# Units 8 to 23 of a recurrence: scores and state stacked into one matmul, one TensorE task per unit

## The chip, the cores and the metric

The program runs on one core of a Trainium2 chip. The metric is device microseconds of that core: 506.9 before (median of 3 runs, 506.85 to 506.91). Below, TensorE is the matmul engine, VectorE, ScalarE and GpSimd the three others that compute, and SyncE (SP) issues most DMAs. SBUF is the memory on the chip, PSUM the eight accumulator banks that TensorE writes.

## The reference

```python
B, H, S, D = 4, 8, 768, 48                 # batch, heads, time, head size
for t in range(S):                         # per batch and head: a 48 x 48 state
    y[t]  = r[t] @ (state + outer(u * k[t], v[t]))
    state = w[t][:, None] * state + outer(k[t], v[t])
x = y as [3072 tokens, 384]
h = x @ w_in                               # 384 x 2048
out = elu(h) @ w_out                       # 2048 x 384
```

All in float32. The decay w lies between 0.8 and 0.95.

## The kernel before, in words

**The recurrence** is computed in blocks of time. There are NU = 24 units. Units 0 to 3 ("whole") are one batch and 128 steps; units 4 to 23 are two batches (halves h = 0, 1, on token rows 0 to 63 and 64 to 127) and 64 steps, and alternate between two pairs of batches, so that unit i + 2 needs the state that unit i leaves. For a unit VectorE makes the running products of w (`e_scan`, `g_scan`) and scales k and r with them (`hats`). Heads stand in four pairs p; q is the head in a pair, on partitions 0 to 47 and 64 to 111.

Of a unit of 64 steps TensorE then computes two tasks. The *score* task `("s", i)` (function `score`): four transposes of k into bank pb (they become `kt`, ScalarE), 16 score matmuls k by r into pa, and the first half of the part of y that comes from the state (`state_part`, 16 matmuls st by r). VectorE writes the scores over the diagonal in tile `am`, where a mask allows it (`mask`; the diagonal, r k u, is spread out by GpSimd in `spread`). The *value* task `("v", i)` (`value`): 32 matmuls of v by am, the second half of the state part, all accumulated in one y, and 16 matmuls kt by v for the state's update. Units 22 and 23 (`last`) have neither transposes nor update. Then y is copied out in two parts, xh (ScalarE) and xl (VectorE, the rest), and the update is added to the state `st` (`update`), which is scaled for unit i + 2 by `scale_state`. A matmul that reads 48 or 64 partitions and writes 32 or 64 uses only a tile of TensorE's 128x128 array (64x32, 64x64), and matmuls in different tiles run side by side. In the trace an fp32 matmul is two instructions (a transpose is one).

**The two layers** run in 6 chunks of 512 tokens, four units each. A step f of 16 is a task g1 (9 matmuls of 128x512, weights and x in two parts each) and a task g2 (9 more); between them ScalarE and VectorE compute the elu (lines 269 to 283). Chunk 0 begins in plain fp32 while the weights are unpacked on ScalarE and VectorE.

**The order** is written out by a planner in the program (class `Plan`): each task has an engine, a cost (`COST`), what it comes after, buffers that it holds (`hold`, `SLOTS`) and, for some, a due time (`BEGINS`, the planned starts of the chunks, and `NUDGE`, a shift for single tasks). The engines get their tasks in the order in which the planner's own clock starts them, and each engine, and SP's queue of DMAs, works through its list in order. Units of chunk c + 1 are thus mixed into the steps of chunk c, and loads start `LEAD` us ahead of their chunk's planned start.

PSUM: three banks acc for the second layer, two ph for the first, two pa, one pb.

Of the kernel before, what the change touches and what calls it, by code (L numbers as in the profile page):

```python
# [20 lines left out]
P = 128  # L21
C = 128
# [25 lines left out]
def _pieces():  # L48
    res = []
    for h in range(H):  # L50
        s, e = h * D, (h + 1) * D
        while s < e:
# [12 lines left out]
            gh=0.62, sp=1.4, s=1.64, s0=1.6, s2=1.1, v=1.95, v0=1.6, v2=1.3, g=2.04, g32=2.65, out=0.6)  # L65
# [4 lines left out]
BEGINS = (21.0, 116.0, 196.0, 274.0, 351.0, 427.0, 493.0)  # L70
# [8 lines left out]
LEAD = 69.5  # L79
# [3 lines left out]
SLOTS = dict(wx=1, w=2, k=3, rk=2, v=3, eg=2, md=2, am=2, kt=2, pa=1, pb=1, wg=2, ph=2, m=2, gh=2, gl=2, x=2, acc=1, raw0=1, raw1=1, x0=1, x1=1, x1a=1, x1b=1)  # L83

LEADS = dict(ld="ld_w ld_k ld_v ld_rk ld_wx", es="es gs", rh="rkc rh kh pc sc", sp="rk rku md pd sp", fl="fl", s="s mk kt", v="v xf xh xl up", raw="raw", a="a",
             cc="cand cs cb cc cx sg", wl="wh wl wt wl1 wh1", g1="g1 r1 r2 stt", g2="g2 gh gl")
NUDGE = dict(a={1: -20.75, 2: -37.25},
             cc={1: -10, 2: -20.25, 6: 56.75, 8: -22, 11: 6, 12: 5.75, 14: -4.75, 15: 1.5},
             es={2: -12.5, 4: 3, 6: 3.5, 7: 13.5, 13: -11.5, 16: -1.75, 20: 3.75},
             g1={3: -1.25, 4: 21, 5: 16.5, 31: -17.25, 37: 70.75, 46: 48.25, 47: -20.75, 48: -0.5, 58: -15.25, 76: -6.25, 80: -9.25, 84: -11.5, 94: -11.75},  # L90
             g2={3: 88.5, 18: 4.25, 19: 14.25, 20: -1.5, 26: -11.5, 33: -5.25, 34: -2.75, 42: 0.25, 43: 6, 48: 24, 54: 7.5, 79: -12.75, 83: -8.5, 84: -17.5, 85: 16.75, 87: -4.25, 94: 6.75, 99: 51.75},
             ld={5: -17.75},
             raw={2: -71.5},
             rh={2: -16, 4: -9.75, 8: -40, 9: -5.5, 17: 42, 19: 17.75},
             s={1: -4.25, 12: 31.25, 17: 10},
             sp={1: 13.25, 6: 3.25, 13: -19.75, 19: -3.25, 23: -6},
             v={8: 24.25, 15: -15.5, 16: -18.25},
             wl={1: -22.25, 8: 15.75, 12: -2.25})
# [3 lines left out]
class Plan:  # L102
# [16 lines left out]
    def order(self):  # L119
# [36 lines left out]
        while len(order) < len(ts):  # L156
            moved = False
            for e in ready:
# [18 lines left out]
                for p, n, us in self.holds.get(k, ()):  # L177
                    at_, n_ = ring[p][0], len(ring[p][1])
                    ring[p][0] = (at_ + n) % n_
                    for x in range(n):  # L180
                        ring[p][1][(at_ + x) % n_] = True
                    if p in turn:
                        turn[p].pop(0)
                        if not turn[p]:
                            del turn[p]
                    h = [p, [(at_ + x) % n_ for x in range(n)], set(us) | {k}]
                    if p == "pa":
# [139 lines left out]
def rwkv_elu_kernel(ctx, tc, wkr, rk, vp, u, uz, gkrw, gv, gu, wraw, out):  # L327
# [39 lines left out]
    xf = xp.tile([P, NK, N], F32, name="xf")  # L367
# [30 lines left out]
    def pair(u_):  # L398
        if u_["i"] in SPARE:
            return spare()[0:2]  # L400
        t = ps_a.tile([P, 2, N], F32, tag="pa", name="pa", bufs=1)
        return [t[:, q] for q in range(2)] if u_["whole"] else t

    def single():
        return ps_a.tile([P, 512], F32, tag="pb", name="pb", bufs=1)
# [14 lines left out]
    def load(u_, n):  # L420
        i = u_["i"]
        if n in WKR:
            lo, hi = WKR[n]
            t, src = ld.tile([R2, hi - lo], F32, tag=n, name=n, bufs=SLOTS[n]), wkr[i, :, lo:hi]
        elif n == "wx":
            t, src = ld.tile([R2, W1], F32, tag=n, name=n, bufs=SLOTS[n]), wkr[i, :, 0:W1]
        elif n == "rk":
            t, src = ld.tile([P, 2, DM], F32, tag=n, name=n, bufs=SLOTS[n]), rk[i]
        else:
            t, src = ld.tile([P, 4 * P], F32, tag=n, name=n, bufs=SLOTS[n]), vp[i]  # L430
# [54 lines left out]

    def spread_act(u_):
        u_["am"] = am = at.tile([P, 2, NP, u_["L"]], F32, tag="am", name="am", bufs=SLOTS["am"])
        for q in range(2):
            for p in range(NP):
                act(am[:, q, p], ident if u_["whole"] else ident_h, AF.Copy, scale=u_["md"][:, q, p:p + 1])  # L490

    def spread_dve(u_):
        u_["am"] = am = at.tile([P, 2, NP, u_["L"]], F32, tag="am", name="am", bufs=SLOTS["am"])
# [3 lines left out]
    def spread(u_):  # L497
        u_["am"] = am = at.tile([P, 2, NP, L], F32, tag="am", name="am", bufs=SLOTS["am"])
        for lo in range(0, P, L):
            rs = slice(lo, lo + L)  # L500
            nc.gpsimd.affine_select(out=am[rs].rearrange("t q p s -> t (q p) s"),  # L501
                                    in_=u_["md"][rs].rearrange("t q p -> t (q p)").unsqueeze(2).broadcast_to([L, NS, L]),
                                    pattern=[[0, NS], [1, L]], compare_op=ALU.is_equal,
                                    fill=0.0, base=0, channel_multiplier=-1)

# [12 lines left out]
    def score(u_):  # L518
        if not u_["last"]:
            u_["pt"] = pt = single()[:, 0:NP * R2].rearrange("t (p d) -> t p d", p=NP)  # L520
            for p in range(NP):
                nc.tensor.transpose(pt[:, p], u_["k"][:, p, :], ident[0:R2, 0:R2])  # L522
        both = pair(u_)
        n = NP * u_["L"]
        if u_["whole"]:
            u_["pa"] = pa = [t[:, 0:n].rearrange("t (p s) -> t p s", p=NP) for t in both]
        else:
            u_["pa"] = both[:, :, 0:n].rearrange("t q (p s) -> t q p s", p=NP)
            pa = [u_["pa"][:, q] for q in range(2)]
        for p in range(NP):  # L530
            for lo in range(0, C, u_["L"]):
                for q in range(2):
                    rs, ts = slice(64 * q, 64 * q + D), slice(lo, lo + u_["L"])
                    nc.tensor.matmul(pa[1 - q][ts, p], u_["k"][rs, p, ts], u_["r"][rs, p, ts], start=True, stop=True)  # L534
        if u_["whole"]:
            u_["pu"] = both[1][0:R2, 0:NP * D].rearrange("d (h p e) -> d h p e", h=1, p=NP)
            u_["py"] = both[0][:, 0:NK * C].rearrange("d (h k t) -> d h k t", h=1, k=NK)
        else:
            u_["pu"] = both[0:R2, :, 0:NP * D].rearrange("d h (p e) -> d h p e", p=NP)
# [3 lines left out]
    def mask(u_):  # L543
        if u_["whole"]:
            for q in range(2):
                nc.vector.copy_predicated(u_["am"][:, q], above[u_["L"]][:, q], u_["pa"][q])
        else:
            nc.vector.copy_predicated(u_["am"], above[u_["L"]], u_["pa"])
# [9 lines left out]
    def value(u_):  # L558
        v, am, kt, whole = u_["v"], u_["am"], u_.get("kt"), u_["whole"]
        rows = [slice(0, C)] if whole else [slice(L * h, L * h + L) for h in range(2)]  # L560
        for n, (p, x) in enumerate(VALUES):
            for h, rs in reversed(list(enumerate(rows))):
                job(u_, h, p, x, v[rs, P * p + 32 * x:P * p + 32 * x + 32], am[rs, 1 - x // 2, p],
                    start=(whole and n < 4), stop=(whole and n >= len(VALUES) - 4))
        if not whole:
            state_part(u_, 0, u_["last"])
        if u_["last"]:
            return
        for p in range(NP):
            for z in range(2):  # L570
                lo = 64 * z
                for h, rs in enumerate(rows):
                    nc.tensor.matmul(u_["pu"][lo:lo + D, h, p], kt[rs, p, lo:lo + D], v[rs, P * p + 80 * z:P * p + 80 * z + D],  # L573
                                     start=whole, stop=(whole or p == NP - 1))
# [103 lines left out]
    for u_ in units:  # L678
# [37 lines left out]
        add(("s", i), "PE", K["s0" if u_["whole"] else "s2" if u_["last"] else "s"], lambda u_=u_: score(u_), [("rh", i), ("const",)] + [("sp", i)] * (i > 1) + before, due=DUE.get(i))  # L716
        add(("mk", i), "DVE", K["mk0" if u_["whole"] else "mk"], lambda u_=u_: mask(u_), [("s", i), ("sp", i)])
        if not u_["last"]:
            add(("kt", i), "ACT", K["kt"], lambda u_=u_: trans_out(u_), [("s", i)])
        after = [("mk", i), ("kt", i), ("ld_v", i)]  # L720
        if i % B:
            after.append(("v", i - 1))
        add(("v", i), "PE", K["v0" if u_["whole"] else "v2" if u_["last"] else "v"], lambda u_=u_: value(u_), after,
# [30 lines left out]
    for c in range(NC):  # L754
# [3 lines left out]
        for f, lo, hi in steps[c]:  # L758
# [17 lines left out]
            if c == NC - 1 and final:  # L776
# [11 lines left out]
                add(("g2", n - 1), "PE", g * 2 / 3 * CUT / N, lambda x=x, y=y: rest(x, y, a, lambda: pair(units[-1])[:, 0], "a"), [("g2a", 2)], due=due)  # L788
# [23 lines left out]
    for u_ in units:  # L812
        i, c = u_["i"], u_["c"]
        for n, users in dict(w=["es", "gs"] + ["fl"] * (i >= LATE), k=["s", "v"], rk=["md"], v=["v"], wx=["fl"]).items():
            hold(n, ("ld_" + n, i), [(x, i) for x in users])
        hold("eg", ("es", i), [("rh", i), ("pc", i)])
# [5 lines left out]
        hold("pb", ("s", i), [("kt", i)], fifo=False)  # L822
        hold("kt", ("s", i), [("v", i)])
        if i not in SPARE:
# [10 lines left out]
    for c in range(NC):  # L835
        hold("raw0", ("out", c, 0), [("store", c, m) for m in range(NK)])
    add(("least",), "DVE", 0.5, least, [(n, i) for i in range(NU) for n in ("fl", "pc")], due=BEGINS[-2] + 10.0)
    add(("guard",), "PE", 0.2, guard, [("least",)], due=BEGINS[-2] + 14.0)
    add(("verdict",), "DVE", 0.35, verdict, [("guard",)], due=BEGINS[-2] + 18.0)
    hold("pb", ("guard",), [("verdict",)], fifo=False)  # L840
    with tc.manual_schedule():
        for t in plan.order():
            warm(FILL.get(t["key"], 0))
# [138 lines left out]
```

## Time and profile before

| | |
|---|---|
| median of 3 runs | 506.9 us |
| the profiled execution | 507.46 us, its span (first to last instruction) 505.7 us |
| TensorE busy | 496.8 us (98%), granted clock 1.0 throughout |
| VectorE, ScalarE, GpSimd busy | 339.0 (67%), 271.4 (54%), 41.2 us (8%) |
| DMA | 51.09 MB in 18738 packets, 33% of the 16 engines' time on the main queue |

The profile is one execution. An engine is busy while one of its instructions runs; matmuls overlap, so a TensorE that is always busy need not be at its peak, and starts say more than durations. In a row of the timeline the first number is the start, the second the time until the last of the group has ended. Line numbers are those of the kernel before.

### The profile page before, as it was taken

What the parts mean: (1) busy time and instruction counts of PE and PEld (TensorE: products, weight loads), DVE (VectorE), ACT (ScalarE), POOL (GpSimd) and SP (SyncE); (2) the same over time, 40 slices, a digit from 0 to 9 for tenths busy, and PEclk for the clock granted to TensorE, in tenths of its full rate; (3) what the DMA queues carried; (4) which work ended last, traced back from release to release, by engine and by line L of the source; (5) the groups of instructions that cost most, each with busy time, mean ns of one, the idle gap of its engine ahead of it and who ended that gap; (6) DMA issues with size and microseconds to landing.
All of it is one profiled execution on the core that took longest, in us unless ns stands there. A gap on an engine that the chain in (4) does not pass through costs nothing.

```text
span 505.7 us, 13790 instructions
## 1 busy us (share of the span) xinstructions
PE 496.8 (98%) x6038; PEld 409.1 (81%) x6038; DVE 339.0 (67%) x509; ACT 271.4 (54%) x526; POOL 41.2 (8%) x54
## 2 busy tenths in 40 slices
PE   8999999999999999999899999999999999999996
PEld 7887888887888788888788888888888887888885
DVE  7999999995997524899432799533799543333332
ACT  4999576657554425655643645444644444445352
POOL 2000000013111100112000031100021100000000
PEclk9999999999999999999999999999999999999999
DMA  8977935204813100844390242230332000100001
GB/s 256 335 229 241 298 128 187 78 4 162 222 50 108 41 3 1 242 128 113 85 249 17 81 121 71 71 98 1 121 100 60 3 0 3 64 3 0 1 0 66
DMA packets 18738, 51.09 MB, mean 101 GB/s; under 512 B 2288, under 2 KB 2416, under 8 KB 18672
## 3 DMA queue, kind: packets, MB, share of 16 engines
q1 hardware_dynamic: 18240, 49.36, 32.7%
q8 instruction: 49, 0.80, 0.6%
q10 hardware_dynamic: 432, 0.79, 0.4%
q14 instruction: 17, 0.14, 0.1%
HBM read 45.42 MB, written 4.72 MB: 99 GB/s over the span
## 4 chain that ended last, share of the span: by engine, by line
PE 88%; DVE 5%; DMA 4%; issue 1%; ACT 1%; DVEq 0%; ACTq 0%
PE acc L296 35%; PE ph L265 34%; PE pa L508 6%; DMA wx<-in_wkr_dram 3%; PE acc L293 3%; PE ph L261 2%; PE pa L534 2%; PE pa L573 2%; PE acc L415 1%; PE pb L522 1%; DVE eg L441 1%; ACT wx L460 1%; DVE eg L451 1%; DMA w<-in_wkr_dram 1%; DVE m L275 1%
## 5 line engine op out<-in xcount | busy, mean ns | idle before, releaser
L275 DVE SCALAR_TENSOR_TENSOR m<-m,ph 128x512 f32<-128x512 f32 (+2 forms) x104 | 66.5, 641 | 82.5 <-ACT m L272 82.2
L269 ACT ACTIVATE m<-ph 128x512 f32<-128x512 f32 (+2 forms) x104 | 58.5, 563 | 92.6 <-PE ph L265 85.2
L265 PE MATMUL ph<-xh,w_l 128*128 128x512 f32 x270 | 105.3, 390 | 0.0
L296 PE MATMUL acc<-gh,w_l 128*128 128x512 f32 x268 | 104.5, 390 | 0.0
L283 DVE TENSOR_TENSOR gl<-m,gh 128x512 fp32r<-128x512 f32 x90 | 62.6, 696 | 42.7 <-ACT gh L279 42.5
L279 ACT CAST gh<-m 128x512 fp32r<-128x512 f32 x90 | 55.7, 619 | 51.5 <-DVE m L275 29.8
L296 PE MATMUL acc<-gh,w_h 128*128 128x512 f32 x180 | 71.8, 399 | 0.0
L265 PE MATMUL ph<-xh,w_h 128*128 128x512 f32 x180 | 71.3, 396 | 0.0
L296 PE MATMUL acc<-gl,w_h 128*128 128x512 f32 x180 | 70.2, 390 | 0.0
L265 PE MATMUL ph<-xl,w_h 128*128 128x512 f32 x180 | 70.1, 389 | 0.0
L272 ACT ACTIVATE m<-m 128x512 f32<-128x512 f32 (+2 forms) x104 | 62.2, 599 | 2.1
L265 PEld LDWEIGHTS ph<-xh,w_l 128*128 128x128 f32 x270 | 50.7, 188 | 10.7
L296 PEld LDWEIGHTS acc<-gh,w_l 128*128 128x128 f32 x268 | 50.3, 188 | 10.7
L501 POOL TENSOR_SCALAR_AFFINE_SELECT am<-md 64x512 f32<-64x512 f32 x32 | 30.3, 947 | 248.7 <-DVE md L470 203.0
L265 PEld LDWEIGHTS ph<-xh,w_h 128*128 128x128 f32 x180 | 33.8, 188 | 7.9 <-DVE m L275 0.6
L296 PEld LDWEIGHTS acc<-gh,w_h 128*128 128x128 f32 x180 | 33.8, 188 | 7.8
L265 PEld LDWEIGHTS ph<-xl,w_h 128*128 128x128 f32 x180 | 33.8, 188 | 6.7
L296 PEld LDWEIGHTS acc<-gl,w_h 128*128 128x128 f32 x180 | 33.8, 188 | 6.5
L265 PE MATMUL ph<-xh,w_g 128*128 128x512 f32 x90 | 36.1, 402 | 0.0
L265 PE MATMUL ph<-xl,w_g 128*128 128x512 f32 x90 | 35.1, 390 | 0.0
L296 PE MATMUL acc<-gh,w_g 128*128 128x512 f32 x88 | 35.1, 398 | 0.0
L296 PE MATMUL acc<-gl,w_g 128*128 128x512 f32 x88 | 34.4, 391 | 0.0
(115 smaller groups left out, 689.1 us busy)
## 6 DMA issues: line engine op xcount, KB each, us to landing
wraw<-in_wraw_dram SPq DMA_DIRECT2D x16, 768.0 KB, 7.1
k<-in_wkr_dram SPq DMA_DIRECT2D x24, 448.0 KB, 6.3
rk<-in_rk_dram SPq DMA_DIRECT2D x20, 384.0 KB, 4.4
v<-in_vp_dram SPq DMA_DIRECT2D x24, 256.0 KB, 7.1
w<-in_wkr_dram SPq DMA_DIRECT2D x24, 227.9 KB, 4.1
out_dram<-o SPq DMA_DIRECT2D x15, 256.0 KB, 2.3
wx<-in_wkr_dram SPq DMA_DIRECT2D x8, 227.9 KB, 3.3
out_dram<-o ACTq DMA_DIRECT2D x3, 256.0 KB, 2.6
```

The source lines that it names most:

```text
L261: nc.tensor.matmul(ph, w_f[f][:, 0, k], x_[2][:, k], start=(k == 0), stop=(k == NK - 1))
L265: nc.tensor.matmul(ph, w[f][:, 0, k], y[:, k], start=(k == n == 0), stop=(k == NK - 1 and n == 2))
L269: act(s["m"], s["ph"], AF.Relu, scale=-1.0)
L272: act(s["m"], s["m"], AF.Exp, scale=-1.0)
L275: stt_(s["m"], s["m"], -1.0, s["ph"], ALU.add, ALU.max)
L279: nc.scalar.copy(s["gh"], s["m"])
L283: nc.vector.tensor_tensor(s["gl"], s["m"], s["gh"].bitcast(F32), ALU.subtract)
L293: nc.tensor.matmul(a_, w_f[f][:, 1, m], fold(s, s["m"][:, a:b]), start=first, stop=final)
L296: nc.tensor.matmul(a_, w[f][:, 1, m], fold(s, g[:, a:b]), start=(first and n == 0), stop=(final and n == 2))
L501: nc.gpsimd.affine_select(out=am[rs].rearrange("t q p s -> t (q p) s"), in_=u_["md"][rs].rearrange("t q p -> t (q p)").unsqueeze(2).broadc ...
L508: nc.tensor.matmul(u_["py"][32 * j:32 * j + 32, h, k], l, r, **flags)
L534: nc.tensor.matmul(pa[1 - q][ts, p], u_["k"][rs, p, ts], u_["r"][rs, p, ts], start=True, stop=True)
```

## The change

For units 8 to 23 (`STACK = 8`) the state part and the values become one matmul. A tile `stack` holds for each half h the 64 rows of v and, on 48 of the other 64 partitions, the scaled state; the 16 rows between are zero (`clear`). The tile am (now `ams`, double width) holds in the same partitions the masked scores and a copy of the decayed r. So `stacked` needs 32 matmuls that read 112 or 128 partitions and write 32 (128x32 tiles) for both halves. v is loaded straight into the stack (two DMAs), and r and the scaled state are put in by four DMAs each from SBUF to SBUF on SP's queue (`copy_r`, `copy_state`).

There is one TensorE task per unit, ("v", i): the scores of unit i + 1, the update of unit i, the stacked matmuls of unit i. Unit 8 alone has a score task of its own. The transposes are a task of their own ("tr", i). The mask is two copies of 64 partitions. y stands in the bank that the transposes use; the three banks are one tile px. The planner knows the new tasks, costs and holds, loads may start 110 us ahead instead of 69.5, and all nudges are new.

Besides: units 4 to 7 run the update first, then values and state; heads of a pair are no longer swapped in am; `stack`, the v buffers of units 0 to 7 and xf share one tile `wide`; and warming matmuls (`FILL`, on ones) are left out behind the first g2 task.

```diff
-BEGINS = (21.0, 116.0, 196.0, 274.0, 351.0, 427.0, 493.0)
+BEGINS = (21.0, 114.0, 191.0, 266.5, 342.0, 417.5, 483.5)
-LEAD = 69.5
+LEAD = 110.0
+STACK = 8
...
+    wide = xp.tile([P, 6 * N], F32, name="wide")
+    xf = wide[:, 0:NK * N].rearrange("p (k n) -> p k n", k=NK)
+    stack = wide.rearrange("p (s h n) -> p s h n", s=3, h=2)
+    ams = cst.tile([P, 2, 2 * NP * C], F32, name="ams")
+    px = ps_a.tile([P, 3, N], F32, name="px")
...
+            u_["stack"] = stack[:, (i - STACK) % 3]
+            for h in range(2):
+                nc.sync.dma_start(u_["stack"][L * h:L * h + L, h], vp[i, L * h:L * h + L])
...
+    def clear(w):
+        nc.gpsimd.memset(stack[32:64, w, 1], 0.0)
+
+    def copy_r(u_):
+        for h in range(2):
+            for q in range(2):
+                nc.sync.dma_start(u_["am"][L - L * h:L - L * h + D, h, q], u_["r"][L * q:L * q + D, :, L * h:L * h + L])
+
+    def copy_state(u_):
+        for h in range(2):
+            for q in range(2):
+                w = u_["stack"][L - L * h:L - L * h + D, h].rearrange("d (p q e) -> d p q e", p=NP, q=2)
+                nc.sync.dma_start(w[:, :, q], st[L * q:L * q + D, u_["b"].start + h, :, 16 - 16 * q:80 - 16 * q])
...
     def score(u_):
+        if u_["i"] >= STACK:
+            scores(u_, halves())
+            return
...
     def mask(u_):
...
+            for h in range(2):
+                rs = slice(L * h, L * h + L)
+                nc.vector.copy_predicated(u_["am"][rs, h], above[L][rs], pa[rs])
...
+    def stacked(u_):
+        i, w = u_["i"], u_["stack"]
+        ahead = i + 1 < NU
+        if ahead:
+            scores(units[i + 1], halves(), close=u_["last"])
+        if not u_["last"]:
+            u_["pu"] = px[0:R2, 0:2, NP * L:NP * L + NP * D].rearrange("d h (p e) -> d h p e", p=NP)
+            update_part(u_, [w[:, h] for h in range(2)], start=False, stop=NP - 1)
+        u_["py"] = px[:, 2, 0:2 * NK * L].rearrange("d (h k t) -> d h k t", h=2, k=NK)
+        for h in range(2):
+            rs = slice(0, P if h else R2)
+            for n, (p, x) in enumerate(VALUES):
+                job(u_, h, p, x, w[rs, h, P * p + 32 * x:P * p + 32 * x + 32], u_["am"][rs, h, x // 2, p],
+                    start=(h == 0 and n < 4), stop=(h == 1 and n >= len(VALUES) - 4))
...
+        if new:
+            add(("rc", i), "SP", 4 * DMA_ISSUE, lambda u_=u_: copy_r(u_), [("rh", i), ("sp", i)], size=K["drc"])
+            add(("tc", i), "SP", 4 * DMA_ISSUE, lambda u_=u_: copy_state(u_), [("ld_v", i)] + before, size=K["dtc"])
+            if not u_["last"]:
+                add(("tr", i), "PE", K["tr"], lambda u_=u_: transposes(u_), [("rh", i)] + [("xl", i - 1), ("xh", i - 1)] * (i > STACK))
...
+        if new:
+            after += [("rc", i), ("tc", i), ("rh", i + 1)] + [("up", i - 1)] * (i > STACK)
...
+            if i == STACK:
+                hold("pa", ("s", i), [("mk", i)], fifo=False)
+            hold("pa", ("v", i), [("up", i), ("mk", i + 1)], fifo=False)
+            hold("pb", ("v", i), [("xh", i), ("xl", i)], fifo=False)
...
-            warm(FILL.get(t["key"], 0))
+            begun = begun or t["key"] == ("g2", 0)
+            warm(0 if begun else FILL.get(t["key"], 0))
```

## Rows read from the trace of the kernel before

**Rows 1.** The page's part 1: busy time, share of the span, instructions.
```profile
PE 496.8 (98%) x6038; PEld 409.1 (81%) x6038; DVE 339.0 (67%) x509; ACT 271.4 (54%) x526; POOL 41.2 (8%) x54
```
**Rows 2.** Busy time by stretch; columns as in the first line.
```profile
core 0: us, PE busy (x) PEld busy (x) DVE busy (x) ACT busy (x) POOL busy (x), PEclk, DMA share, GB/s
66.00:117.00 51.00, 51.00 (x949) 41.30 (x948) 49.99 (x74) 34.53 (x58) 3.39 (x3) 1.00 0.26 83
117.00:425.00 308.00, 306.12 (x4032) 249.02 (x4034) 199.44 (x301) 150.86 (x293) 33.48 (x36) 1.00 0.31 88
```
**Rows 3.** Timeline of TensorE (start, us, ...): starts of the value tasks of units 8, 9, 10.
```profile
157.35 0.81 PE L508 MATMUL pa<-am,v 64*32 64x64 f32 x61
...
165.52 0.80 PE L508 MATMUL pa<-am,v 64*32 64x64 f32 x61 [0.56 <-issue]
...
177.12 0.81 PE L508 MATMUL pa<-am,v 64*32 64x64 f32 x61
```
**Rows 4.** TensorE's waits from 20 to 500 us: total, times, longest.
```profile
PE pa L508 <- DVE am L548: 1.3, 1, 1.3
PE pa L508 <- issue: 0.6, 1, 0.6
PE ph L261 <- DVE m L275: 0.4, 1, 0.4
```
**Rows 5.** Timeline of TensorE: a score task.
```profile
80.32 0.55 PE L522 MATMUL pb<-ident,k 112*128 112x112 f32 x4
80.80 0.69 PE L534 MATMUL pa<-k 48*64 48x64 f32 x32
81.42 0.45 PE L508 MATMUL pa<-k,st 48*32 48x64 f32 x32
81.81 0.50 PE L296 MATMUL acc<-gh,w_h 128*128 128x512 f32 x1
82.14 0.39 PE L296 MATMUL acc<-gl,w_h 128*128 128x512 f32 x1
```
**Rows 6.** Timeline of TensorE: the value task of the same unit.
```profile
83.76 0.39 PE L296 MATMUL acc<-gh,w_l 128*128 128x512 f32 x1
84.07 0.81 PE L508 MATMUL pa<-am,v 64*32 64x64 f32 x61
...
84.73 0.51 PE L508 MATMUL pa<-k,st 48*32 48x64 f32 x30
85.18 0.57 PE L573 MATMUL pa<-v,kt 64*48 64x48 f32 x32
85.68 0.50 PE L265 MATMUL ph<-xh,w_h 128*128 128x512 f32 x1
```
**Rows 7.** Timeline of TensorE: values and update of a whole unit.
```profile
17.20 1.08 PE L508 MATMUL pa<-am,v 128*32 128x128 f32 x32
18.21 0.56 PE L573 MATMUL pa<-v,kt 128*48 128x48 f32 x16
18.71 0.38 PE L415 MATMUL acc<-ones 128*128 128x128 f32 x1
```
**Rows 8.** The mask's line: count, ns min/median/max, first and last start.
```profile
L548 DVE COPY_PREDICATED am<-upper_h,pa x20: 719/736/755, 82.6 to 426.2; 128x512 f32<-128x512 uint32 x20
```
**Rows 9.** SP's timeline, an issue; then the page's part 6: KB, us to landing.
```profile
120.73 0.44 SPq L431 DMA_DIRECT2D w<-in_wkr_dram  x1
...
v<-in_vp_dram SPq DMA_DIRECT2D x24, 256.0 KB, 7.1
...
out_dram<-o SPq DMA_DIRECT2D x15, 256.0 KB, 2.3
```
**Rows 10.** VectorE's timeline: unit 8's state added, and scaled for unit 10.
```profile
160.08 0.54 DVE L601 TENSOR_TENSOR st<-st,pa 112x384 f32<-112x384 f32 x1
...
161.15 0.55 DVE L556 TENSOR_TENSOR st<-st,pcs 112x384 f32<-112x384 f32 x1
```
**Rows 11.** The page's part 5: GpSimd's spread (busy, mean ns).
```profile
L501 POOL TENSOR_SCALAR_AFFINE_SELECT am<-md 64x512 f32<-64x512 f32 x32 | 30.3, 947 | 248.7 <-DVE md L470 203.0
```
**Rows 12.** Timeline of TensorE: the last warming matmuls.
```profile
24.00 1.36 PE L415 MATMUL acc<-ones 128*128 128x128 f32 x10
```

More of the change, by code (lines that the diff above doesn't have):

```diff
@@ L400, in pair @@
             return spare()[0:2]
-        t = ps_a.tile([P, 2, N], F32, tag="pa", name="pa", bufs=1)
-        return [t[:, q] for q in range(2)] if u_["whole"] else t
+        return [px[:, q] for q in range(2)] if u_["whole"] else px[:, 0:2]
     def single():
-        return ps_a.tile([P, 512], F32, tag="pb", name="pb", bufs=1)
+        return px[:, 2]
     def spare():
@@ L492, in spread_dve @@
     def spread_dve(u_):
-        u_["am"] = am = at.tile([P, 2, NP, u_["L"]], F32, tag="am", name="am", bufs=SLOTS["am"])
+        am = diagonal(u_)
         i_, m_ = ident if u_["whole"] else ident_h, u_["md"].rearrange("t q p -> t (q p)")
@@ L497, in spread @@
     def spread(u_):
[L498 to L501, printed above, removed]
+        am = diagonal(u_)
+        for h in range(2):
+            rs = slice(L * h, L * h + L)
+            nc.gpsimd.affine_select(out=am[rs, h].rearrange("t q p s -> t (q p) s"),
                                     in_=u_["md"][rs].rearrange("t q p -> t (q p)").unsqueeze(2).broadcast_to([L, NS, L]),
@@ L516, in state_part, with transposes, scores @@
                     stop=(stop and n >= 2 * NP - 4))
[L518 to L529, printed above, removed]
+    def transposes(u_):
+        u_["pt"] = pt = single()[:, 0:NP * R2].rearrange("t (p d) -> t p d", p=NP)
+        for p in range(NP):
+            nc.tensor.transpose(pt[:, p], u_["k"][:, p, :], ident[0:R2, 0:R2])
+    def scores(u_, pa, each=False, close=True):
         for p in range(NP):
@@ L533, in score, with halves @@
                     rs, ts = slice(64 * q, 64 * q + D), slice(lo, lo + u_["L"])
-                    nc.tensor.matmul(pa[1 - q][ts, p], u_["k"][rs, p, ts], u_["r"][rs, p, ts], start=True, stop=True)
+                    nc.tensor.matmul(pa[q][ts, p], u_["k"][rs, p, ts], u_["r"][rs, p, ts], start=each or p == 0, stop=each or (close and p == NP - 1))
+    def halves():
+        t = px[:, 0:2, 0:NP * L].rearrange("t q (p s) -> t q p s", p=NP)
+        return [t[:, q] for q in range(2)]
+    def score(u_):
+        if u_["i"] >= STACK:
+            scores(u_, halves())
+            return
+        if not u_["last"]:
+            transposes(u_)
+        both = pair(u_)
+        n = NP * u_["L"]
         if u_["whole"]:
+            u_["pa"] = [t[:, 0:n].rearrange("t (p s) -> t p s", p=NP) for t in both]
+            scores(u_, u_["pa"], True)
             u_["pu"] = both[1][0:R2, 0:NP * D].rearrange("d (h p e) -> d h p e", h=1, p=NP)
@@ L538, in score @@
         else:
+            scores(u_, halves()[::-1], True)
             u_["pu"] = both[0:R2, :, 0:NP * D].rearrange("d h (p e) -> d h p e", p=NP)
@@ L543, in mask @@
     def mask(u_):
+        pa = px[:, 0:2, 0:NP * L].rearrange("t q (p s) -> t q p s", p=NP)
         if u_["whole"]:
@@ L556, in scale_state, with update_part @@
         tt(sv[:, b], sv[:, b], u_["pc"].rearrange("d (p h) o -> d h p o", h=2).broadcast_to([R2, 2, NP, D]), ALU.mult)
[L558 to L568, printed above, removed]
+    def update_part(u_, v, **flags):
+        rows = [slice(0, C)] if u_["whole"] else [slice(L * h, L * h + L) for h in range(2)]
         for p in range(NP):
@@ L572, in value @@
                 for h, rs in enumerate(rows):
-                    nc.tensor.matmul(u_["pu"][lo:lo + D, h, p], kt[rs, p, lo:lo + D], v[rs, P * p + 80 * z:P * p + 80 * z + D],
-                                     start=whole, stop=(whole or p == NP - 1))
+                    nc.tensor.matmul(u_["pu"][lo:lo + D, h, p], u_["kt"][rs, p, lo:lo + D], v[h][rs, P * p + 80 * z:P * p + 80 * z + D],
+                                     **{n: x if isinstance(x, bool) else p == x for n, x in flags.items()})
+    def value(u_):
+        v, am, whole = [u_["v"]] * 2, u_["am"], u_["whole"]
+        rows = [slice(0, C)] if whole else [slice(L * h, L * h + L) for h in range(2)]
+        if not whole and not u_["last"]:
+            update_part(u_, v, start=False, stop=False)
+        for n, (p, x) in enumerate(VALUES):
+            for h, rs in enumerate(rows):
+                job(u_, h, p, x, v[h][rs, P * p + 32 * x:P * p + 32 * x + 32], am[rs, x // 2, p],
+                    start=(whole and n < 4), stop=(whole and n >= len(VALUES) - 4))
+        if whole:
+            update_part(u_, v, start=True, stop=True)
+        else:
+            state_part(u_, 0, True)
+    def stacked(u_):
[7 more added lines that the diff above has]
+        u_["py"] = px[:, 2, 0:2 * NK * L].rearrange("d (h k t) -> d h k t", h=2, k=NK)
+        for h in range(2):
+            rs = slice(0, P if h else R2)
+            for n, (p, x) in enumerate(VALUES):
+                job(u_, h, p, x, w[rs, h, P * p + 32 * x:P * p + 32 * x + 32], u_["am"][rs, h, x // 2, p],
+                    start=(h == 0 and n < 4), stop=(h == 1 and n >= len(VALUES) - 4))
     def columns(u_, t):
@@ L813, in rwkv_elu_kernel @@
         i, c = u_["i"], u_["c"]
-        for n, users in dict(w=["es", "gs"] + ["fl"] * (i >= LATE), k=["s", "v"], rk=["md"], v=["v"], wx=["fl"]).items():
+        new = i >= STACK
+        if new:
+            kus = [("rc", i), ("tr", i), ("s", i) if i == STACK else ("v", i - 1)]
+        else:
+            kus = [("s", i), ("v", i)]
+        for n, users in dict(w=["es", "gs"] + ["fl"] * (i >= LATE), rk=["md"], wx=["fl"]).items():
             hold(n, ("ld_" + n, i), [(x, i) for x in users])
+        hold("k", ("ld_k", i), kus)
+        hold("stack" if new else "v", ("ld_v", i), [("v", i)])
+        if new:
+            plan.tasks[("ld_v", i)]["after"].append(("clear", (i - STACK) % 3))
         hold("eg", ("es", i), [("rh", i), ("pc", i)])
@@ L836, in rwkv_elu_kernel @@
         hold("raw0", ("out", c, 0), [("store", c, m) for m in range(NK)])
+    for w in range(3):
+        done = [("xl", i) for i in range(B)] + [("g1", n) for n, x in enumerate(steps[0]) if x[0] < K32]
+        add(("clear", w), "POOL", 0.5, lambda w=w: clear(w), done + [("v", i) for i in range(B, STACK) if (3 + i % 3) // 2 == w], lock=True)
     add(("least",), "DVE", 0.5, least, [(n, i) for i in range(NU) for n in ("fl", "pc")], due=BEGINS[-2] + 10.0)
```

81 lines of the change are left out of this document (49 added, 32 removed).

## The prediction

> **What bounds the kernel now.** I read the page's busy times first [rows 1]: TensorE is busy 496.8 of 505.7 us. A share near one can still hide waits, so the stretches come next [rows 2]: from 66 to 117 us TensorE lacks nothing, from 117 to 425 only 1.9 of 308 us, and the granted clock is 1.00, the 2.4 GHz level. VectorE is as full as TensorE up to 117 us (50.0 of 51), then it has 199.4 of 308. Units 8 to 23 come in that second stretch, the first of them at 157.35 us [rows 3]. The list of TensorE's waits [rows 4] has three entries after 20 us, 2.3 us together, the longest 1.3 for a mask (am). So what is taken out of TensorE's queue after 117 us comes off the end, and what is added there is paid.
>
> **A unit before.** The timeline gives starts, and a group's cost is from its start to the next group's. MLP matmuls start 0.23 us apart. The score task [rows 5] has 4 transposes (80.32 to 80.80, 0.48), scores (to 81.42, 0.62), the first state half (to 81.81, 0.39), and the first MLP matmul behind it takes 0.33 (to 82.14), 0.10 over normal: 1.59. The value task [rows 6] begins 0.08 late (83.76 + 0.23 = 83.99, then 84.07), values take 0.66 (to 84.73), the second state half 0.45 (to 85.18), the update 0.50 (to 85.68), and I give the MLP matmul behind it the same 0.10: 1.79. Together 3.38 us. Units 22 and 23 have no transposes (1.11) and no update (1.29): 2.40.
>
> **A unit after.** 32 state and 32 value matmuls in 64-row tiles become 32 matmuls in 128x32 tiles. Each fp32 matmul is two instructions in the rows, so 128 become 64. The question is what 64 of them take, with 64 columns each on four tiles: 16 rounds of four. No row shows this form with 64 columns. The whole units show it with 128 [rows 7]: 32 instructions, 8 rounds, 1.01 us (17.20 to 18.21), and next to them 128x48 tiles with 48 columns, two at a time, also 8 rounds, 0.50 us (to 18.71). A line through both has 0.0064 us per column for 8 rounds and a constant of 0.19. For 8 rounds of 64 columns it gives 0.60, and the score group of such rounds is 0.62. So 16 rounds of 64 take 0.82 + 0.19 = 1.01. From above: values and state now need 1.11 us for 12 rounds (96 instructions on eight tiles, 0.66 + 0.45), 0.092 a round, so 1.48. I take 1.10, near the rows of the same tile form.
> Of the constant 0.19 I put 0.10 down to the change of tile form, an estimate from the extras beside the MLP (0.08 and 0.10). Scores of the next unit and the update now stand side by side in one form, so one such change goes: scores 0.52 (between 0.43 and 0.62), update 0.50. The task is 0.08 + 0.52 + 0.50 + 1.10 + 0.10 = 2.30. The transposes stand alone between MLP matmuls of the same full-array form: 0.42 (between 0.38, the change gone, and 0.58, one more). Sum 2.72, a saving of 0.66.
> Units 9 to 21 are 13: 8.6 us. Unit 8 also pays a score task of its own (0.08 + 0.62 + 0.10) and loses 0.14. Unit 22 takes 0.08 + 0.62 + 1.10 + 0.10 = 1.90 and saves 0.50. Unit 23 takes 1.28 and saves 1.12. TensorE's work shrinks by 10.1 us. With the ends of the stacked part alone, 0.92 (the line without the change) and 1.48, it is 13.0 and 4.0.
>
> A rule of the Trainium skill speaks against the new form. Its page "TensorE: Matmul & The Clock Gate", Part 3 (The mechanism), says that a weight load overlaps running matmuls only when its row group differs, and in 128-row tiles all tiles share all row groups. The row to hold against it is the 128x48 group [rows 7]: its tiles share the row groups too, and with 48 columns it needs half of what the 128-column group needs, so there the loads don't set the pace. By the rule the sum would be that of rival 2; by the row it stays.
>
> **What is beside TensorE.** All of the following I cost at nothing, with its cover.
> - Masks: one 128-row predicated copy of 0.74 us [rows 8] becomes two of 64 rows, 0 to 0.74 more per unit (0 if half the rows took half). 16 times 0.74 is 11.8 us on VectorE, which has 108 us free from 117 to 425 us [rows 2]. Without that cover it would be up to 0.74 on each unit's way; but a unit's scores are now made one unit earlier, so its mask has a whole unit's spacing. The 1.3 us wait for a mask [rows 4] should go; another may take its place, so I count 0.5 of it.
> - DMAs: per unit 4 for decayed r, 4 for the scaled state and 2 instead of 1 for v, 9 more on SP's queue at an issue of some 0.44 us [rows 9]: 4 us per unit, 63 in all, on a queue that only issues. Queued behind a copy that waits for the state's scaling are the next units' loads; these may start 110 instead of 69.5 us ahead of their chunk, and k and stack have three buffers. If the loads were late, TensorE would wait with them, as in rival 3.
> - The state's way is the tight one: unit 8's value task starts at 157.35, its state is added by 160.62 and scaled for unit 10 by 161.70 [rows 10]; unit 10 needs it at 177.12 [rows 3]. That leaves 15.4 us for 4 issues (1.8) and a landing, 2.3 to 7.1 us for transfers of 256 KB [rows 9]: 6.5 us of slack. The new task is 0.5 us longer than the old value task, which leaves 6.
> - r's way: GpSimd rebuilds am after the value task that read it, two instructions of 0.95 us [rows 11], and then these copies have till 177.12 as well.
> - The new task holds the bank of the transposes until ScalarE and VectorE have read x. The state's sum, which comes behind those reads, is done 3.3 us after the start of the value task [rows 10], and the nearest next unit starts 8.2 us after it [rows 3].
> - Clearing (three memsets) is GpSimd's, with 33.5 of 308 us in that stretch [rows 2].
> - For units 4 to 7 the update stands ahead of the values: the same instructions, 0.1 either way for each.
> - Warming matmuls are dropped behind the first second-layer task. The last ones before (10 instructions, 1.2 us at 24.00 [rows 12]) stand ahead of it, so nothing goes unless the order turns: 0 to 1.2.
> - All due times and nudges change, and the order of MLP tasks with them. The waits after 20 us sum to 2.3 us, so little can be won by order; I allow up to 3 lost.
>
> **Sum.** Span 505.7 - 10.1 - 0.5 = 495.1. The profiled execution took 507.46, 1.8 more than its span, so 496.9 by it; the median of 506.9 stands 0.6 below that execution: 496.3.
>
> **Rivals.**
> 1. The stacked part runs at the pace of the 64-row tiles, 1.48: 0.38 more 16 times, 502.4. For it: the value and state rows are the only ones with 64 columns into 32-column tiles. Against: there eight tiles share the issue, here four. Chance 0.13.
> 2. A round doesn't get shorter with its columns, since weight loads in 128-row tiles wait: 16 rounds at 0.126 (1.01 / 8) are 2.02, 0.92 over my value, 14.7 in all: 511, slower. It decides from 1.76 us on, 0.11 a round. For it: this form has been seen with 128 columns only; against it the 48-column group. (It is the page's rule above.) Chance 0.04.
> 3. Copies land late. Where the state's way takes 6 us more than the 8.9 reckoned, TensorE waits ahead of the stacked part; with 0.66 us of wait per unit the gain is gone, with 1.4 the time is 508. For it: the copies go in pieces of 256 bytes (64 fp32 values), far smaller than the pieces of the loads of k, v and w. Against: the DMA share is 0.31 from 117 us on [rows 2]. Chance 0.06, half of it slower than before, half between 497 and 506. The Trainium skill ("DMA: Bandwidth & Descriptors", Specifications) asks for transfers of 512 bytes or more for full rate; no run here shows that yet.
> 4. The order also closes the last waits and drops the warming matmuls: 2 to 3 us better, 494. Chance 0.15.
>
> My forecast has 0.62, with a range of its own of 494.5 to 499.5. Over all cases, 492.8 to 502.5 leaves out about 2 in 10 (the slow cases, part of rival 1 and the best of rival 4). About 0.2% (1 us) can be told from no change: faster 0.92, same 0.02, slower 0.06.
>
> **What would show it.** Right: no state rows of units 8 to 23 in a score task; a stacked group of 1.0 to 1.2 us; the update right behind scores; 2.3 us for the task; TensorE busy for about 486 us, its waits still below 3. Wrong: a wait of TensorE that a DMA into am or stack ends (rival 3), stacked groups of 1.5 or 2.0 (rivals 1 and 2), or VectorE full after 117 us.

## The result and the profile after

509.3 us (median of 5 runs, 508.95 to 510.34) against 506.9 for the kernel before (5 runs): ratio 1.0058, 95% interval 1.0042 to 1.0073. The change makes the kernel 0.6% slower; the forecast was 496.3. The profiled execution took 509.03, its span 507.3 (before 507.46 and 505.7).

The page's part 1 of the changed kernel, beside [rows 1]:

```profile
PE 490.3 (97%) x5014; PEld 401.8 (79%) x5014; DVE 351.9 (69%) x525; ACT 273.1 (54%) x526; POOL 42.8 (8%) x57
```
TensorE has 1024 instructions fewer and is busy 6.5 us less, in a span that is 1.6 us longer. Busy time by stretch, beside [rows 2]:

```profile
core 0: us, PE busy (x) PEld busy (x) DVE busy (x) ACT busy (x) POOL busy (x), PEclk, DMA share, GB/s
66.00:117.00 51.00, 50.94 (x827) 40.70 (x825) 50.48 (x76) 35.58 (x59) 0.98 (x2) 1.00 0.49 153
117.00:425.00 308.00, 300.78 (x3288) 243.41 (x3288) 215.15 (x321) 153.52 (x296) 36.95 (x38) 1.00 0.38 100
```
From 117 to 425 us TensorE now stands still for 7.2 of 308 us (before 1.9). VectorE has 15.7 us more work there. The granted clock is unchanged at 1.00. TensorE's waits from 20 to 500 us (total, times, longest), beside [rows 4], say where it stands still:

```profile
PE px L553 <- DVE st L668: 2.5, 3, 1.3
PE px L553 <- DVE ams L595: 2.0, 2, 1.1
PE ph L267 <- DVE m L277: 1.5, 2, 0.9
PE ph L263 <- DVE m L277: 1.5, 3, 0.9
PE acc L298 <- DVE gl L285: 0.4, 1, 0.4
PE px L553 <- DVE xl L660: 0.4, 1, 0.4
```
8.3 us against 2.3 before. Most of it, 4.9 us, stands ahead of the transposes (L553), and no DMA ends any of it. What ends it is odd: the state's sum (L668) and the mask (L595) read the first two banks of px, and the transposes write the third. ScalarE waits in the same way where it copies x out of the third bank (its waits from 66 to 500 us):

```profile
ACT xh L656 <- DVE ams L595: 23.4, 5, 8.3
```
Both the copy and the mask only read px, and they read different banks.

**The task itself is as small as forecast.** The timeline of TensorE (start, us until the group has ended), a whole task of the changed kernel, to be held against [rows 5] and [rows 6]:

```profile
136.51 0.39 PE L298 MATMUL acc<-gh,w_l 128*128 128x512 f32 x1
136.83 0.69 PE L560 MATMUL px<-k 48*64 48x64 f32 x32
137.35 0.54 PE L611 MATMUL px<-wide,kt 64*48 64x48 f32 x32
137.82 1.10 PE L540 MATMUL px<-ams,wide 112*32 112x64 f32 x64
138.85 0.50 PE L298 MATMUL acc<-gh,w_h 128*128 128x512 f32 x1
139.19 0.39 PE L298 MATMUL acc<-gl,w_h 128*128 128x512 f32 x1
```
From start to start: 0.09 of delay, scores 0.52, update 0.47, the stacked part 1.03, and 0.11 over normal for the matmul of the layers behind: 2.22 us where 2.30 was predicted.

**A wait at the transposes, from close by.** Timeline of VectorE from 142 to 146 us, then of TensorE; in brackets the idle time before and what ended it:

```profile
142.19 0.55 DVE L660 TENSOR_TENSOR xl<-px,xh 128x384 fp32r<-128x384 f32 x1
142.66 1.47 DVE L595 COPY_PREDICATED ams<-upper_h,px 64x512 f32<-64x512 uint32 x2
144.82 0.55 DVE L668 TENSOR_TENSOR st<-st,px 112x384 f32<-112x384 f32 x1 [0.69 <-PE px L553]
```
```profile
142.84 0.39 PE L267 MATMUL ph<-xh,w_l 128*128 128x512 f32 x1
144.18 0.60 PE L553 MATMUL px<-ident,k 112*128 112x112 f32 x4 [0.95 <-DVE ams L595]
144.56 0.47 PE L267 MATMUL ph<-xh,w_h 128*128 128x512 f32 x1
```
The third bank is free once xl has been read, at 142.7. The transposes start at 144.18, right behind the end of the mask at 144.13. Then the state's sum, whose operands were ready before, starts at 144.82, right behind the transposes. Each waits for a use of banks that it doesn't touch itself. What the three banks share is that they are one tile, px; experiment 1 tests whether that is the cause.

**The end of the program.** VectorE's last two instructions of the changed kernel (one row, x2), TensorE's last matmul, and the transfers from 499.5 to 508 us in 40 slices of 0.21 us:

```profile
501.08 0.76 DVE L312 TENSOR_TENSOR o<-px,part 128x384 f32<-128x384 f32 x2 [1.06 <-PE px L298]
```
```profile
500.70 0.27 PE L298 MATMUL px<-gh,w_l 128*128 128x128 f32 x1
```
```profile
GB/s 77 0 10 337 386 347 97 10 29 270 405 366 212 0 0 386 357 366 126 39 39 0 0 10 10 10 19 29 0 0 0 0 0 0 0 0 0 0 0 0
```
And the same two engines in the kernel before:

```profile
501.09 0.56 DVE L310 TENSOR_TENSOR o<-pa,part 128x384 f32<-128x384 f32 x1 [0.42 <-PE pa L296]
501.64 0.29 DVE L310 TENSOR_TENSOR o<-pb,part 128x128 f32<-128x128 f32 x1
```
```profile
501.33 0.27 PE L296 MATMUL pb<-gh,w_l 128*128 128x128 f32 x1
```
Before, the sum of the first 384 columns (bank pa) runs beside the matmuls of the last 128 (bank pb). After, it starts when they have all ended (500.97). TensorE ends 0.6 us earlier than before and the span ends 1.6 later: 4.1 us lie between the two before, 6.3 after. About 0.5 of that is the late sum. The rest is the last transfer: at 503.5 most of it is through, and then 0 to 39 GB/s trickle until 505.5.

**Where 12.2 us went.** I split TensorE's time from start to start of its matmuls: a step no longer than the usual one for its pair of instructions is work, the excess is loss. This is the table for the kernels below, except that of experiment 4; "end" is from TensorE's last matmul to the end of the span. The 1.3 us that the columns lack lie ahead of the first matmul and in the last one.

| profiled execution | span | work | loss to 66 us | loss from 66 us | end |
|---|---|---|---|---|---|
| before | 505.7 | 484.9 | 6.3 | 9.1 | 4.1 |
| after | 507.3 | 474.1 | 7.8 | 17.8 | 6.3 |
| two tiles | 500.1 | 473.6 | 6.8 | 14.1 | 4.3 |
| two tiles, again | 501.4 | 473.6 | 6.8 | 15.7 | 4.0 |
| after, stacking off | 516.7 | 485.2 | 10.2 | 13.3 | 6.8 |
| two tiles, one mask copy | 502.2 | 473.8 | 10.4 | 12.7 | 4.1 |
| two tiles, mask cost 1.5 | 503.9 | 474.6 | 6.7 | 16.7 | 4.6 |
| two tiles, no nudges | 506.9 | 474.0 | 10.5 | 17.3 | 3.9 |
| two tiles, last sums in one | 502.9 | 473.5 | 6.7 | 15.9 | 5.5 |
| after, last sum elsewhere | 508.0 | 474.1 | 7.4 | 20.6 | 4.5 |
| before, one tile | 508.0 | 484.9 | 7.7 | 8.3 | 5.8 |

Forecast span 495.1, measured 507.3: the work is 0.7 better than forecast (-10.8 for -10.1), the losses between matmuls are 10.7 worse (+10.2 for -0.5), the end is 2.2 worse. What counts as usual is a choice: with a wider allowance (the third quartile of a pair's steps and 0.05 us) the work falls by 9.8 instead of 10.8 us, and the distances from before move by up to 2 us in work and up to 1 in the loss from 66 us. The loss to 66 us differs by 3.6 us between runs whose code is the same there (two tiles 6.8, one mask copy 10.4), so a microsecond of it proves nothing. The loss from 66 us differs by 1.6 between the two runs of the two-tile kernel, and by 2.8 between the changed kernel and experiment 7, whose engines work in the same order up to the last sum.

### The profile page after: what moved, and what is told of

The parts are those of the page before. It is cut to its first block, busy times and chain, and to the rows that moved or that the text cites. A ratio compares the mean times of both kernels' runs of the same rounds, so it can differ in the third digit from the quotient of the medians.

```text
span 507.3 us, 12027 instructions
## 1 busy us (share of the span) xinstructions
PE 490.3 (97%) x5014; PEld 401.8 (79%) x5014; DVE 351.9 (69%) x525; ACT 273.1 (54%) x526; POOL 42.8 (8%) x57
## 4 chain that ended last, share of the span: by engine, by line
## 5 line engine op out<-in xcount | busy, mean ns | idle before, releaser
L267 PE MATMUL ph<-xh,w_h 128*128 128x512 f32 x180 | 72.6, 403 | 0.2
L298 PEld LDWEIGHTS acc<-gh,w_l 128*128 128x128 f32 x268 | 50.3, 188 | 10.4
L519 POOL TENSOR_SCALAR_AFFINE_SELECT ams<-md 64x512 f32<-64x512 f32 x32 | 31.0, 968 | 223.8 <-DVE md L480 105.9
```

The source lines that it names most:

```text
L267: nc.tensor.matmul(ph, w[f][:, 0, k], y[:, k], start=(k == n == 0), stop=(k == NK - 1 and n == 2))
L298: nc.tensor.matmul(a_, w[f][:, 1, m], fold(s, g[:, a:b]), start=(first and n == 0), stop=(final and n == 2))
L519: nc.gpsimd.affine_select(out=am[rs, h].rearrange("t q p s -> t (q p) s"), in_=u_["md"][rs].rearrange("t q p -> t (q p)").unsqueeze(2).bro ...
```

## The experiments

**1. Two tiles instead of one.** px keeps its first two banks, the third is a tile of its own, py. The work is the same, and in the traces each engine's instructions come in the same order.

```diff
-    px = ps_a.tile([P, 3, N], F32, name="px")
+    px = ps_a.tile([P, 2, N], F32, name="px")
+    py = ps_a.tile([P, N], F32, name="py")
...
-        return px[:, 2]
+        return py
...
-        u_["py"] = px[:, 2, 0:2 * NK * L].rearrange("d (h k t) -> d h k t", h=2, k=NK)
+        u_["py"] = py[:, 0:2 * NK * L].rearrange("d (h k t) -> d h k t", h=2, k=NK)
```


> The changed kernel with its three PSUM banks px declared as two tiles (two banks for scores and update, one for transposes and y); the order of every engine's work is the same. Theory F: the transposes wait for VectorE's mask copies and state sums, which touch other banks, only since all three banks are one tile. Then TensorE's waits at the transposes (4.9 us listed, some 5.5 by starts) fall under 1.5, ScalarE's copies of x no longer wait for masks (23.4 us), and the time falls from 509.3 by 5 to 6 us to 503 to 505, below the kernel before (506.9). Rival V: VectorE is late anyway, with the low part of x that the transposes must wait for; then the waits stand at that line instead and the time stays within 1 us of 509.3.

Measured: 502.9 us (6 runs, 501.35 to 503.9), 0.9919 of before (0.9893 to 0.9946). TensorE's waits from 20 to 500 us, and its busy time:

```profile
PE acc L298 <- DVE gl L285: 2.0, 3, 1.3
PE ph L263 <- DVE m L277: 1.4, 3, 0.9
PE ph L267 <- DVE m L277: 1.3, 3, 0.7
PE px L612 <- ACT kt L600: 0.2, 1, 0.2
```
```profile
117.00:425.00 308.00, 304.40 (x3261) 247.20 (x3245) 216.65 (x325) 156.34 (x301) 37.34 (x38) 1.00 0.39 100
```
The waits at the transposes are gone (L554 here has no row), ScalarE's copy of x waits for TensorE alone, and the end is 4.3 us again:

```profile
ACT xh L657 <- PE py L541: 19.3, 7, 6.6
```
One declaration is worth 6.4 us, a little more than the 5 to 6 expected, and turns the change from 0.6% slower to 0.8% faster. Rival V, the same time with other waits, is out. VectorE is as loaded as in the changed kernel (216.65), so its load alone was not what made the change a loss.

**2. The changed kernel without its stacking.** New order, lead and px as one tile, old matmuls.

```diff
-STACK = 8
+STACK = 24
```
(and `spread` takes its old operand where nothing is stacked.)

> The changed kernel with STACK = 24: no unit is stacked, all 64-step units have the two tasks of before, while the new nudges, due times, lead, one PSUM tile, shared tile for v and update-first order stay. Theory F: the old tasks have their transposes inside the score task, which had to wait for the masks and sums before too, so TensorE's stalls behind 66 us return to about 6 us from 13; TensorE's work is 10 us more than in the changed kernel: 509.3 + 10.3 - 6 = 513 to 515. Rival O: the new order costs the stalls whatever the unit looks like: about 519.

Measured: 515.8 us (4 runs, 514.24 to 518.53), 1.0164 of before (1.0128 to 1.0199). The median is 0.8 above theory F's 515, which the interval includes, and 3 below rival O's 519, which it doesn't. No row of TensorE's waits is at the transposes, though px is one tile. But by the table the losses from 66 us on fall by 4.5 (17.8 to 13.3) and not by 7; 4.2 more than before are left with the old tasks. Work is 485.2 us, 11.1 more than with stacking: that is what stacking saves on TensorE. The kernel is slower than before by everything else: the losses (3.9 more to 66 us and 4.2 behind it in the profiled execution, the slowest of the four) and the end (6.8).

**3. Two tiles, second mask copy left out.** The scores of the second half of a unit never reach ams.

```diff
-            for h in range(2):
+            for h in range(1):
                 rs = slice(L * h, L * h + L)
                 nc.vector.copy_predicated(u_["am"][rs, h], above[L][rs], pa[rs])
```


> The two-tile kernel of e1, with the second of the two mask copies of units 8 to 23 left out (the scores of half h = 1 don't enter the result; order and all else the same). Theory D: what keeps e1 at 502 and not 496 are VectorE's results that come late for the layers, and the second copy of 0.74 us per unit is a good part of it. Then the jumps of over 0.15 us between TensorE starts behind 66 us fall from 5.7 to about 3 and TensorE ends some 2 us earlier (495.8 to 494). Rival O: the order of VectorE's list makes them late, not its load: less than 0.7 us.

Measured: 503.9 us in one run, whose start lost 3.6 us more than that of experiment 1, at a granted clock of 0.96 from 20 to 66 us. From 66 us on it loses 12.7, against 14.1 and 15.7 of the two runs of the two-tile kernel. The masks' row from 117 to 425 us in experiment 1 shows what is left out:

```profile
L596 DVE COPY_PREDICATED ams<-upper_h,px 64x512 f32<-64x512 uint32 x32 | 23.5, 735 | 10.6 <-PE px L612 9.9 <-PE px L561 0.2
```
A copy of 64 partitions takes 735 ns, one of 128 took 736 [rows 8], so splitting doubles the masks: 11.8 us for VectorE. Without the second copy TensorE loses 1.4 to 3.0 us less. That agrees with the expected 2 in size, but equal orders differ by 1.6 to 2.8 from run to run, and TensorE ended at 498.1 instead of the expected 494, mostly for the start. So one run only suggests that the second copy costs TensorE something.

**4. Two tiles, loads no earlier than before.**

```diff
-LEAD = 110.0
+LEAD = 69.5
```


> The two-tile kernel of e1 with LEAD back at 69.5 us. Theory S: the 1.9 us that chunk 0 lost before 66 us come from the earlier loads, whose scans crowd VectorE there; with the old lead TensorE's stretch from 20 to 66 us is busy 45.4 us again instead of 44.6, and the time is 1 to 2 us less. Rival N: the nudges were chosen for the new lead, and with the old one the order is worse: 1 to 4 us more.

Measured: 524.3 us in one run, far past both. The nudges stayed those of the long lead, so the run doesn't tell the lead from an order that no longer fits it; with these nudges the change needs the long lead. TensorE's longest waits:

```profile
PE ph L267 <- DVE m L277: 8.6, 9, 2.2
PE ph L263 <- DVE m L277: 3.3, 3, 1.4
PE acc L298 <- DVE gl L285: 3.2, 2, 1.9
PE px L561 <- DVE k L467: 2.5, 1, 2.5
```
VectorE's k and its part of the elu (m, gl) are late. TensorE waits for no transfer itself; VectorE waits once for k (3.2 us) and once for w (2.1 us), against 2.0 for k in experiment 1. TensorE's granted clock was 0.91 from 195 to 272 us, so part of the time may be the clock's.

**5. Two tiles, no nudges.**

```diff
-NUDGE = dict(a={0: -9.92, 1: 11.38, ...}, ...)
+NUDGE = {}
```


> The two-tile kernel of e1 with no nudges at all: how much the order of the tasks is worth here. The prediction allowed 3 us for it. Theory: the planner's order alone costs 3 to 10 us more in waits for VectorE; if it is within 2 us, order isn't what separates e1 from the forecast.

Measured: 508.7 us in one run, 6.8 over the profiled execution of experiment 1; 3.2 of it are lost from 66 us on (1.6 against experiment 10), 3.7 at the start, which also differs between equal kernels, here as in experiment 3 at a clock of 0.96. The time lies in the theory's 3 to 10, but half of it is the start's. From 66 us on the nudges are worth 1.6 to 3.2 us by this one run, and equal orders differ by 1.6 to 2.8.

**6. The kernel before, with one tile.** Nothing of the change but px.

```diff
+    px = ps_a.tile([P, 3, N], F32, name="px")
...
-        t = ps_a.tile([P, 2, N], F32, tag="pa", name="pa", bufs=1)
-        return [t[:, q] for q in range(2)] if u_["whole"] else t
+        return [px[:, q] for q in range(2)] if u_["whole"] else px[:, 0:2]
...
-        return ps_a.tile([P, 512], F32, tag="pb", name="pb", bufs=1)
+        return px[:, 2]
```


> The kernel before with its three banks pa and pb declared as one tile, nothing else. Theory F: there the transposes are part of the score task, which waits for the masks and sums of the unit before anyhow, so TensorE hardly waits more (under 1 us); at the end the first of the last two sums must wait for the last six matmuls, 0.5 us. In all 0.5 to 1.5 us slower than before. Rival G: one tile costs about 5 us in any form of the kernel: 511 to 513.

Measured: 510.2 us (10 runs, 507.54 to 512.25), 1.0072 of before (1.0048 to 1.0096): 3.8 us more, between the two theories. TensorE loses no more from 66 us on (8.3 against 9.1), and no transposes wait. Of the 2.3 us between the profiled executions 1.7 stand in the end (5.8); the 1.4 more at the start prove nothing, as said. So here and in experiment 2, with the old tasks, one tile costs the transposes nothing; it does with the new ones, where y takes the bank of the transposes while masks and update are in the other two. The long end belongs to one tile in any order.

**7. The changed kernel, its last sum out of px.** The last 128 columns go into the third accumulator bank.

```diff
-... lambda x=x, y=y: rest(x, y, b, single, "b"), ...
+... lambda x=x, y=y: rest(x, y, b, lambda fns=fns: fns["accs"]()[2], "b"), ...
```
(and `accs` is handed out with the other functions of the layers.)

> The changed kernel with px still one tile; only the last piece of the second layer (128 columns) goes into the third accumulator bank, a tile of its own, and not into px. Theory T (the end of the program pays for the one tile as well: the first of the two last sums waits for the matmuls of the second, and the last output transfer is issued later): the time from TensorE's last matmul to the end of the span goes from 6.3 back to 4.1 to 4.3 us, the time from 509.3 to about 507.2, with the waits at the transposes unchanged (some 5 us). Rival U (the longer end comes from something else of these kernels, such as where a fetch of instructions falls): the end stays at 5.8 to 6.8 and the time at 509.

**8. Two tiles, with both last sums in px.**

```diff
-... lambda x=x, y=y: rest(x, y, b, single, "b"), ...
+... lambda x=x, y=y: rest(x, y, b, lambda: px[:, 1], "b"), ...
```


> The kernel with two tiles (px of two banks, py), with the last piece of the second layer put into the second bank of px instead of py, so that the last two sums read one tile again. Theory T: the end of the program grows from 4.3 to 5.8 to 6.8 us and the time from 502.9 to about 505; no wait at the transposes. Rival U: the end stays at 4.3 and the time at 502.9.

Measured together: experiment 7 gives 508.3 us (10 runs, 506.27 to 510.17), ratio 1.0017 (0.9985 to 1.0048); experiment 8 gives 505.0 (10 runs, 501.92 to 508.81), ratio 0.9949 (0.9914 to 0.9984). VectorE's last rows, first of 7, then of 8:

```profile
502.92 0.56 DVE L312 TENSOR_TENSOR o<-px,part 128x384 f32<-128x384 f32 x1 [0.44 <-PE px L298]
503.47 0.29 DVE L312 TENSOR_TENSOR o<-acc,part 128x128 f32<-128x128 f32 x1
```
```profile
497.52 0.76 DVE L312 TENSOR_TENSOR o<-px,part 128x384 f32<-128x384 f32 x2 [1.06 <-PE px L298]
```
The end shrinks from 6.3 to 4.5 us in the one and grows from 4.0 (experiment 10) to 5.5 in the other, each within 0.3 of theory T's range and far from its rival's. In time, 8 shows the expected 2.1 over the first measurement of two tiles and 2.4 over the second, though its runs spread over those of both. 7 gains 1.0 on the changed kernel by the medians and 2.1, as expected, by the two ratios, whose intervals overlap a little; so its time proves little. Its waits at the transposes are still there (2.6 and 2.0 us), as expected, and 8 has none.

**9. Two tiles, the planner told of the real masks.**

```diff
-... mk2=1.25, ...
+... mk2=1.5, ...
```


> The kernel with two tiles, and the planner told that the two copies of a mask take 1.5 us (as the traces show) and not 1.25; the order written out changes with it on all engines. If VectorE's lateness for the elu comes from masks that the planner takes as too short, the losses from 66 us on fall from 14.1 to about 11 and the time to 500. Rival N (the nudges fit one order only, and any other is worse): 3 to 8 us slower, 506 to 511.

Measured: 505.6 us in one run, losses from 66 us on 16.7, not 11. One wait is new and long, TensorE for `m` of VectorE, 4.5 us. The time is 2.6 and 3.7 us above the profiled 503.1 and 502.0, near the low end of rival N. Since the whole order changes with the cost, the run shows that this order is no better, and not what the masks' true length would be worth.

**10. Two tiles once more.**

> The same kernel as in the first experiment (two tiles), once more on this chip, beside the other three. About 0.992 of the kernel before, 502 to 504 us, with the end of 4.3 us.

Measured: 502.6 us (4 runs, 501.48 to 503.32), 0.9888 of before (0.9819 to 0.9957), 0.991 by the medians; the end is 4.0 us. The two-tile version is faster than the kernel before on two chips.

## Why the prediction was wrong

**The step that failed** is a bullet among those costed at nothing: "The new task holds the bank of the transposes until ScalarE and VectorE have read x". It counted with separate banks, as pa and pb had been, though the change makes all three one tile. With one tile, a writer of any bank waits for the readers of all three, and a reader for the writers, so the transposes also wait for the masks and the state's sum, the sum waits for the transposes, and the first of the last two sums waits for the matmuls of the second. Readers of different banks take turns as well: ScalarE's copy of x stood behind the mask for 23.4 us in all, and VectorE's xl and with it the transposes come behind that copy; with two tiles no such row is left. The bullet also counted the 8.2 us to the next value task, while the transposes come sooner: 5.4 us behind the start of a task at the shortest in the changed kernel (187.77 to 193.18 us). Two tiles give back 7.2 us of span (6.4 of the medians): 3.7 from 66 us on (2.1 against the second run), 1.0 at the start, 2.0 at the end, 0.5 of work. So of the 12.2 us that the span is over the forecast, 5.9 to 7.2 are the one tile, and 5.0 to 6.3 are left with two. None of the rivals had this mechanism, and none had a price at the program's end, which the sum took over unchanged with the rest of the span.

**The second step** is the order: "up to 3 lost", with 0.5 won in the sum. With two tiles, losses from 66 us on are still 5.0 to 6.6 above those of before. The remaining waits, but for one of 0.2 us, are for VectorE's part of the elu. A stretch of experiment 1 shows one, on VectorE and then on TensorE:

```profile
267.91 1.24 DVE L452 TENSOR_TENSOR_SCAN eg<-w,reset 112x520 f32<-112x520 f32 x1
269.06 0.67 DVE L277 SCALAR_TENSOR_TENSOR m<-m,ph 128x512 f32<-128x512 f32 x1
269.64 0.55 DVE L481 TENSOR_REDUCE md<-rk 128x8 f32<-128x384 f32 x1
270.11 0.68 DVE L285 TENSOR_TENSOR gl<-m,gh 128x512 fp32r<-128x512 f32 x1
```
```profile
270.84 0.50 PE L298 MATMUL acc<-gl,w_g 128*128 128x512 f32 x1 [1.27 <-DVE gl L285]
```
VectorE never idles here; m and gl stand behind a scan and a reduction in its list. The doubled masks may be part of it (experiment 3). The prediction covered them by 108 us of free time on VectorE, an average over 308 us; an engine that works its list in order is late in a stretch that is full, whatever the average. How the rest is shared between this load and the order stays open: the two other orders tried (5, 9) are no better, and a better one was not found. The change also merged buffers in SBUF (`wide`, `ams`); no run takes these apart, but none of TensorE's remaining waits names them.

**What held.** TensorE's work: -10.8 us for -10.1 (its busy time, 490.3 where about 486 was expected, hides part of this: a matmul of the layers counts as busy for 0.39 us while starts are 0.23 apart, so delays up to 0.16 look busy); the stacked part 1.03 for 1.10; scores and update 0.52 and 0.47 for 0.52 and 0.50. So rival 1 (1.48) and rival 2 (2.02) are out. The Trainium skill's rule behind rival 2 ("TensorE: Matmul & The Clock Gate", Part 3, The mechanism: a weight load overlaps running matmuls only where the row group differs) does not fit this form: 64 instructions of tiles that share their row groups start within 1.03 us. Rival 3 is out as well; its price was wrong besides, since 1.4 us of wait in each of 16 units would have made 519 and not 508. Part 6 of the page (KB, median us to landing) has the new copies:

```profile
wide<-st SPq DMA_DIRECT2D x64, 48.0 KB, 2.1
ams<-k SPq DMA_DIRECT2D x64, 48.0 KB, 2.1
```
They land in 2.1 us (median), below the 2.3 to 7.1 allowed, and TensorE never waits for one. The Trainium skill's demand for 512 bytes or more ("DMA: Bandwidth & Descriptors", Specifications) spoke for that rival; at a DMA share of 0.38 these small pieces delay nothing of TensorE's that the trace shows. Rival 4 had the sign of the order's effect wrong.

The mask's wait of 1.3 us [rows 4] did go from the value task, as forecast; it came back ahead of the transposes.

## What to carry to other kernels

Count waits in PSUM by tile, not by bank: in this program three banks merged into one tile made users of one bank wait for users of the others, and each engine's list must be read again with that in mind. When a forecast takes microseconds out of an engine that is 98% busy, look at what the other engines deliver to it in each stretch, not at their mean, and at the instructions behind its last one. Before giving up on a change, try its mere declarations by themselves, such as which buffers share a tile: here one of them decided the sign.

## What the runs showed of the hardware

A copy under a mask takes as long for 64 partitions as for 128 (735 and 736 ns). In the changed kernel the last output transfer trickled for 2 us, at 10 to 29 GB/s at last, by estimate what one of the 16 DMA engines has of the 386 GB/s before (24). Its last eight packets of 2 KB begin at 504.47, when a fetch of instructions (16 KB, 502.75 to 504.48 us) ends, and end 1.8 us after the others. Behind TensorE's last matmul such fetches begin at 1.7 to 2.5 us in all twelve traces. Where the last sums stand in two tiles the output's packets are about through by then (2.2 to 2.4 us, eight traces); with both in one tile the sums end 0.5 us later, and the last packets at 3.2 (experiments 6 and 8) and 4.5 us (the changed kernel, experiment 2). Experiments 7 and 8 tie the longer end to the late sum; that the fetches turn 0.5 us of lateness into 1.5 to 2 is what the order in time suggests, and was not tested by itself.
